# A fused linear-attention and feed-forward kernel: first rows of w loaded apart, w2 cast by its own load, and a new written-out order of the steps

## The chip, the cores and the metric

The kernel runs on one core of one Trainium2 chip. The metric is the device time of one execution in microseconds (us). TensorE (PE) multiplies matrices and writes PSUM; its weight loads (PEld) run beside its multiplications. VectorE (DVE), ScalarE (ACT) and GpSimd (POOL) do elementwise work, and GpSimd cannot read PSUM. DMAs move data between the chip's main memory and SBUF on 16 shared DMA engines. They are issued here by SyncE (SP), which does nothing else, by ACT in between its own instructions, and, in the changed kernel, by GpSimd too.

## The reference, cut to what matters

The first part is a linear attention with a decayed state, per batch b and head h; the second is a layer norm and a two-layer feed-forward block with a residual.

```python
# B, H, S, D = 4, 8, 768, 48
for t in range(S):
    kt, vt, rt = k[:, :, t], v[:, :, t], r[:, :, t]
    cur = einsum('bhd,bhe->bhde', u[None] * kt, vt)
    y[:, :, t] = einsum('bhd,bhde->bhe', rt, state + cur)
    state = w[None, :, :, None] * state + einsum('bhd,bhe->bhde', kt, vt)
x = y.transpose(0, 2, 1, 3).reshape(B, S, 384)
mu, var = mean(x, -1), mean((x - mu) ** 2, -1)
xn = (x - mu) / sqrt(var + 1e-06) * g_ln
out = x + maximum(xn @ w_ch1, 0) @ w_ch2        # w_ch1: 384x1536, w_ch2: 1536x384
```

## The kernel before, in words

The sequence is cut into 24 chunks of 128 positions (6 in each of 4 batches). Everything is a list of small steps, `PLAN`, a text of entries "name,number,engine" that is written out by hand or by a search outside the kernel. The loop at the end walks through it and emits each step. Every engine runs its own steps strictly in the order in which they stand; the text thus fixes five queues, and all DMAs also keep the order of the text among themselves. The engine letter is v for DVE, s for ACT, g for POOL; a DMA step with "s" is issued by ACT, without it by SP.

DMAs from SP and ACT share eight completion semaphores in turn. So a DMA is not issued before the DMA that stands eight places ahead of it in the common order has landed, whichever engine issued that one. The instruction that issues waits, and with it the queue of its engine.

The steps that the text speaks of, in the order of the work on one chunk i:

- LK, LV, LR load k, v, r of a chunk (192 KB each); KA/KB and RA/RB load k and r of a chunk in two "packed" halves of 96 KB. kf, rf and vf have ten slots each.
- SK, SR multiply k and r by powers of the decay (`Fk`, `Fkp`, `Fr`, `Fn`); CV casts v.
- TR transposes both on PE into one PSUM tile; TCr and TCk copy the two halves to `trs`. Later chunks have this done by transposing DMAs (TKD, TKR). For chunks 0 to 3, TB and KC transpose k back.
- Q multiplies the two; AT makes the scores on PE, AM (AMa, AMb in halves) masks them on DVE; S makes the state update and the u-term on PE; CC and VB form the u-term; ZU (and ZD) decay the state; Y makes the attention output on PE; X adds the u-term on DVE.
- SQ and XN center the row and sum its squares, RS makes the reciprocal root on POOL. LT (PE) and XT (copy), or the transposing DMAs LT2 and LTD, make `xT`.
- UP multiplies by w1 (12 or 6 matmuls a step, two PSUM tiles `hp` in turn); RL is the relu into `hT`, on ACT or DVE. DN multiplies by w2: four steps of four matmuls a chunk, the d-th of which reads `w2_sb[d]` (d from 0 to 2), and `hT`. OT (DVE) scales, adds the residual and writes `ot`, STO stores it. `ot` has four slots, the PSUM tile of DN one.
- In the feed-forward part, chunks 0 to 5 and 20 to 23 go alone, those between in pairs.

Before the first chunk can start, the decay powers are made. LC,0 loads w into `rows` (a tile of 11 x 128 that MW fills with ones first, since the 48 values of a head stand in a field of 64); LN takes the logarithm on ACT; WBR spreads it over the partitions on PE; PW, ER and EK (DVE) multiply it by positions, FR and FKP (ACT) take the exponentials. In the same way BD, WBK, FN and FK make the unpacked powers, and CT and CP turn w, u and g into columns for UW, WL and UGC.

The weights: LW1 loads w1 in three parts (n = 0, 1, 2), and nine SW steps scale them by -g into bf16 tiles `w1_sb`, on ACT, DVE and POOL. LW2 loads w2 in three parts of 768 KB as f32 into `w2_f`, and six CW steps cast them to bf16 into `w2_sb` (two each on POOL, DVE and ACT). The 31 DU steps are dummy matmuls on PE.

Lines of the profile: L236 WBR, L248 and L250 LC, L226 LN, L309 DU, L371 LW1, L388 LW2, L378/L380/L382 SW, L211/L213 copies and casts on ACT/DVE and POOL, L216 products (Q, SK, SR, Z), L400 packed loads, L396 LK, L427 LV, L448 and L452 TR, L479 AT, L489 AM, L523 S, L560 Y, L567 X, L574 SQ, L580 XN, L599 LT2, L611 TKD, L631 UP, L647/L649 RL on ACT/DVE, L659 DN, L715 OT, L722 STO.

Of the kernel before, what the change touches and what calls it, by code (L numbers as in the profile page):

```python
# [18 lines left out]
SLOTS = {'kf': 10, 'rf': 10, 'vf': 10, 'sc': 3, 'vv': 4, 'trs': 3, 'q': 2, 'A': 2, 'cc': 4, 'Z': 6, 'ZS': 2, 'Vb': 3, 'x': 13, 'xn': 4, 'xT': 4, 'hT': 4, 'ot': 4}  # L19
# [16 lines left out]
AM,5,v VB,4,v UP,48,- DN,8,- TR,6,- DN,9,- UP,50,- S,5,- TCk,6,v X,4,v TCr,6,s CC,5,v RL,48,v SK,8,g SR,8,g DN,10,- SQ,4,s
CV,5,s VB,5,g CV,6,s XN,4,s AT,6,- OT,2,v TR,8,- Y,5,- UP,49,- AM,6,v TCk,8,s X,5,v DN,12,- TCr,8,s RL,49,v LK,9,- RB,10,s
RL,50,s Q,6,g SR,7,v XN,5,v AT,8,- Y,6,- LT,4,- S,6,- DN,13,- XT,4,s SK,7,g LV,9,- RA,10,- RA,13,- LT,5,- UP,64,- XT,5,v
SQ,3,s RS,4,g Q,8,v CC,6,s SR,9,g RS,3,g STO,0,- TR,7,- DN,14,- ZU,6,v AM,8,v OT,3,v UP,80,- RL,64,s TCr,7,s CV,7,s TCk,7,s
UP,66,- Q,7,v AT,7,- VB,6,g SK,9,g TR,9,- S,7,- AM,7,v ZU,7,v X,6,v CC,7,v RL,80,s TCk,9,s TCr,9,s DN,16,- UP,65,- LK,10,-  # L40
RA,15,- LV,8,- RB,11,- RB,13,- SR,10,g Q,9,v VB,7,v ZD,7,v AT,9,- Y,7,- CV,9,g RL,66,s RL,65,s SK,10,g XN,6,s CV,8,s TR,10,-
UP,81,- X,7,v SR,11,v DN,17,- XN,7,s TCr,10,s S,8,- LK,11,- SQ,5,s RL,81,s DN,18,- ZU,8,v TCk,10,v CC,8,v RA,12,- LK,12,- UP,82,-
OT,4,v SK,11,g S,9,- TR,11,- DN,20,- ZD,8,g AM,9,v ZU,9,v VB,8,v CC,9,v Y,8,- SR,13,g DN,21,- RS,5,g LV,10,- LV,13,- RL,82,s
STO,1,s TCr,11,s AT,10,- CV,10,s SQ,6,s LT2,6,- RB,14,- RB,12,- X,8,v ZD,9,g SK,12,g VB,9,g LK,14,- LV,11,- DN,22,- Y,9,- UP,96,-
LK,13,- SQ,7,s TCk,11,v SR,12,g RA,16,s UP,97,- AM,10,v RB,15,- AT,11,- RL,96,v XN,8,s Q,10,v X,9,v RL,97,s UP,99,- S,10,- Y,10,-
UP,101,- LV,12,- RA,14,- OT,5,v TR,12,- XN,9,g SQ,9,s RL,99,s RL,101,s UP,98,- CC,10,v ZU,10,v Q,11,v UP,100,- DN,24,- SK,14,g SK,13,g
TCr,12,s TCk,12,s RL,100,s S,11,- LT2,8,- VB,10,g RB,16,- STO,5,- TR,13,- AM,11,v SR,14,v LK,15,- RS,6,g CV,12,v RL,98,s ZD,10,g TCr,13,s
# [12 lines left out]
RL,165,v TKR,20,- LR,22,- X,17,v AM,18,v CV,19,v DN,48,- UP,162,- S,18,- STO,8,s XN,17,s SQ,15,s CC,18,s DN,49,- AT,19,- DN,50,- Q,19,v  # L60
ZU,18,v OT,12,v S,19,- UP,164,- Y,18,- RL,162,s AM,19,v DN,52,- VB,18,g SK,22,g LT2,16,- UP,161,- STO,9,- CV,20,s CC,19,s ZU,19,v X,18,v
# [16 lines left out]
def kernel(  # L78
# [316 lines left out]
    def LK(i, e):  # L395
        nc.sync.dma_start(out=kf(i)[:], in_=chunk_src(k, i))  # L396
# [375 lines left out]
```

## Time and profile before

| | |
|---|---|
| median of 3 runs | 154.98 us (153.17 to 155.23) |
| profiled execution | 154.51 us, its span 152.4 us |
| granted TensorE clock, mean | 0.985 |
| bytes moved, read and written in main memory | 27.75 MB; 18.88 MB, 4.72 MB |

"Span" runs from the first to the last instruction; about 2 us lie around it. Shares and busy times are those of the page of the profile, which describes one execution. In its second part the span is cut into 40 slices of 3.8 us, with the busy share of each engine in tenths. The chain of waits follows the work that ended last back through what released it.

### The profile page before, as it was taken

The numbers are of one execution on the slowest core, as the hardware profiler recorded it, in microseconds if no ns is written. First come the engines' busy times: TensorE is split into PE (matmuls) and PEld (weight loads), VectorE is DVE, ScalarE is ACT, GpSimd is POOL, SyncE is SP. The second block draws the span as 40 slices with busy tenths as digits, with TensorE's granted clock in tenths as the row PEclk, the third lists the DMA queues.
The fourth block names the chain that finished last, engine by engine and source line by source line (L and its number), as shares of the span: only waits on it lengthen the run. The fifth ranks groups of instructions, "written<-read, shape, count | busy, mean of one in ns | idle before, by whom it ended". The sixth has DMA issues, their size and how long they took to land.

```text
span 152.4 us, 4469 instructions
## 1 busy us (share of the span) xinstructions
PE 142.4 (93%) x1755; PEld 109.8 (72%) x1755; DVE 120.9 (79%) x247; ACT 80.8 (53%) x178; POOL 90.9 (60%) x129
## 2 busy tenths in 40 slices
PE   7669799999999999999997899999999999999991
PEld 1235388786878887989785778887777787888880
DVE  0585889969997989999885989997999697674631
ACT  3226787977197787697545373666463514331010
POOL 5216526842999939999997057694839917622000
PEclk9995999999999999999999999999999999999998
DMA  5999998798686857959799599999888894042103
GB/s 179 244 232 305 369 426 240 159 217 192 133 215 139 195 114 176 225 150 242 124 175 203 124 185 215 182 214 176 217 181 162 193 209 147 3 131 85 48 14 141
DMA packets 79394, 27.75 MB, mean 182 GB/s; under 512 B 69003, under 2 KB 77838, under 8 KB 79374
## 3 DMA queue, kind: packets, MB, share of 16 engines
q1 hardware_dynamic: 77040, 25.11, 70.7%
q10 hardware_dynamic: 2334, 2.36, 4.8%
q8 instruction: 13, 0.21, 0.6%
q14 instruction: 7, 0.06, 0.1%
HBM read 18.88 MB, written 4.72 MB: 155 GB/s over the span
## 4 chain that ended last, share of the span: by engine, by line
PE 76%; DMA 12%; DVE 4%; SPq 2%; ACT 1%; issue 1%; POOL 1%; DVEq 0%; ACTq 0%
PE o L659 29%; PE hp L631 29%; DMA w_f<-in_moe_w_ch_dram 4%; PE at L479 4%; DMA out_dram<-ot 3%; PE y L560 3%; DMA vf<-in_v_dram 2%; DMA rows<-in_w_dram 2%; PE y L552 2%; PE tr L448 2%; PE s L523 2%; PE tr L452 2%; PE s L510 1%; SPq L400 1%; DVE w_sb L213 1%; ACT w_sb L378 1%
## 5 line engine op out<-in xcount | busy, mean ns | idle before, releaser
L659 PE MATMUL o<-w_sb,hT 128*128 128x384 bf16 x276 | 55.7, 326 | 1.8 <-DVE ot L715 1.5
L631 PE MATMUL hp<-xT,w_sb 128*128 128x128 bf16 (+1 forms) x612 | 57.1, 241 | 0.0
L631 PEld LDWEIGHTS <-w_sb 128*128 128x128 bf16 x612 | 48.8, 113 | 4.1
L647 ACT ACTIVATE hT<-hp 128x512 bf16<-128x512 f32 x51 | 29.8, 596 | 30.7 <-PE hp L631 22.1
L659 PEld LDWEIGHTS <-hT 128*128 128x128 bf16 x276 | 24.1, 98 | 12.8 <-issue 1.7
L489 DVE TENSOR_TENSOR A<-at,mask 128x1024 bf16<-128x1024 f32 (+1 forms) x27 | 29.7, 1099 | 2.1 <-PE at L479 2.0
L216 POOL TENSOR_TENSOR q<-trs 128x512 bf16<-128x512 bf16 x13 | 15.1, 1165 | 15.4 <-PE s L510 4.8
L715 DVE SCALAR_TENSOR_TENSOR ot<-o,rs,x 128x384 f32<-128x384 f32 x23 | 14.1, 615 | 10.8 <-PE o L659 7.9
L211 ACT COPY trs<-tr 128x512 bf16<-128x512 bf16 x25 | 13.8, 585 | 10.6 <-PE tr L452 3.3
L216 POOL TENSOR_TENSOR sc<-kf,Fk 128x384 bf16<-128x384 f32 x15 | 15.9, 1064 | 3.8 <-PE s L523 3.6
L542 POOL TENSOR_TENSOR Vb<-vf,cc 128x384 f32<-128x384 f32 x16 | 13.7, 858 | 7.4 <-ACT cc L211 3.9
L574 ACT ACTIVATE sqj<-x,sm 128x384 bf16<-128x384 f32 x24 | 14.8, 615 | 3.9 <-DVE x L567 3.3
L649 DVE TENSOR_SCALAR hT<-hp 128x512 bf16<-128x512 f32 x21 | 14.3, 688 | 2.0 <-PE hp L631 1.6
L567 DVE SCALAR_TENSOR_TENSOR x<-y,Vb 128x384 f32<-128x384 f32 x24 | 13.2, 550 | 2.1 <-PE y L560 1.6
L309 PE MATMUL o<-warm 128*128 128x512 bf16 x31 | 11.3, 468 | 1.1 <-DVE warm L264 1.1
L580 ACT ACTIVATE xn<-x,sm 128x384 bf16<-128x384 f32 x13 | 7.9, 611 | 7.3 <-DVE x L567 7.3
L591 POOL TENSOR_TENSOR rs<-rs,expo 128x1 f32<-128x1 f32 (+1 forms) x17 | 10.9, 642 | 1.4
L216 POOL TENSOR_TENSOR sc<-rf,Fr 128x384 bf16<-128x384 f32 x9 | 10.0, 1114 | 0.9 <-DMA rf<-in_r_dram 0.9
L479 PE MATMUL at<-trs 48*128 48x128 bf16 x192 | 9.8, 222 | 0.0
L479 PEld LDWEIGHTS <-trs 48*128 48x128 bf16 x192 | 5.6, 95 | 5.0 <-issue 3.9
L211 ACT CAST vv<-vf 128x384 bf16<-128x384 f32 x14 | 7.1, 513 | 3.9 <-DMA vf<-in_v_dram 3.1
L560 PE MATMUL y<-vv,A 128*128 128x48 bf16 x192 | 8.9, 183 | 0.1
(100 smaller groups left out, 190.0 us busy)
## 6 DMA issues: line engine op xcount, KB each, us to landing
w_f<-in_moe_w_ch_dram SPq DMA_DIRECT2D x6, 768.0 KB, 7.7
vf<-in_v_dram SPq DMA_DIRECT2D x24, 192.0 KB, 3.5
kf<-in_k_dram SPq DMA_DIRECT2D x20, 192.0 KB, 3.6
rf<-in_r_dram SPq DMA_DIRECT2D x30, 96.0 KB, 3.1
out_dram<-ot SPq DMA_DIRECT2D x15, 192.0 KB, 3.3
out_dram<-ot ACTq DMA_DIRECT2D x8, 192.0 KB, 3.1
rf<-in_r_dram SPq DMA_DIRECT2D x6, 192.0 KB, 3.6
kf<-in_k_dram SPq DMA_DIRECT2D x7, 96.0 KB, 3.4
```

The lines of the kernel that those rows point to most:

```text
L211: nc.scalar.copy(out=out, in_=in_)
L216: engines[e].tensor_tensor(out=out, in0=in0, in1=in1, op=ALU.mult)
L479: nc.tensor.matmul(out=t[:, par, q, :], lhsT=trs(i)[p0 : p0 + D, 1, q, :], rhs=trs(i)[p0 : p0 + D, 0, q, :], start=True, stop=True,)
L489: nc.vector.tensor_tensor(out=AA(i)[:, a:b].rearrange("p e q t -> p (e q) t"), in0=psum["at", i][:, a:b].rearrange("p e q t -> p (e q) t") ...
L542: engines[e].tensor_tensor(out=Vb(i)[:].rearrange("p (h d) -> p h d", h=H), in0=vf(i)[:], in1=cc(i)[:].unsqueeze(2).to_broadcast([P, H, D] ...
L560: nc.tensor.matmul(out=t[:, h * D : (h + 1) * D], lhsT=AA(i)[:, par, q, :], rhs=vv(i)[:, h, :], start=first, stop=True, skip_group_check=True,
L574: nc.scalar.activation(out=sqj[:], in_=xx(i)[:], func=ACT.Square, bias=sm[i][:], scale=-float(C), accum_out=sq[g][:, j : j + 1])
L631: nc.tensor.matmul(out=t[:, a * gw : (a + 1) * gw].rearrange("p (j t) -> p j t", j=size), lhsT=w1_sb[n][kc][:, fb::FB], rhs=xT(g)[:, :size ...
L647: nc.scalar.activation(out=o, in_=s, func=ACT.Relu)
L649: nc.vector.tensor_relu(out=o, in_=s)
L659: nc.tensor.matmul(out=psum["o", i][:, :C], lhsT=hT(g)[:, fk, j * P : (j + 1) * P], rhs=w2_sb[d][:, a, :], start=(fk == 0), stop=(fk == FK ...
L715: nc.vector.scalar_tensor_tensor(out=ot(i), in0=psum["o", i][:, :C], scalar=rs[g][:, j : j + 1], in1=xx(i)[:], op0=ALU.mult, op1=ALU.add,)
```

## The change

- LC,0 still loads w into `rows`, for the columns. But a new step LE, the first of the text, loads w once more into a tile of its own, `w_rows` of 4 x 96 (two heads of 48 in a row, no gap), from SP. LN reads that; `ln_rows` shrinks from 129 to 97 columns, and BD, WBR, PW and the spreading products with it.
- The three LW2 loads and the six CW casts are gone, and with them the f32 staging tiles. Three steps IW2, DMAs issued by GpSimd that read f32 and write bf16, put w2 straight into `w2_sb`. They take none of the eight semaphores.
- `hT` gets six slots in place of four.
- LK, LR and LV may be issued by ACT. ACT issues 47 DMAs in place of 18, among them LV,0, KA,0, KB,0, LV,1 and KA,2 at the start.
- The text of `PLAN` is a new one, 888 entries in place of 894, with 30 dummies in place of 31. The attention and feed-forward steps are the same in kind and number; their order and many engines are not. On DVE: Q 20 (was 11), SK 11 (8), SR 8 (14), RL 17 (21), CC 11 (18), ZD 2 (5), TCr and TCk 4 (7), XN 3 (4). On POOL: Q 4 (13), SR 16 (10), SK 13 (16), CV 9 (4), ZD 10 (7), XN 5 (7).

The core of the diff:

```diff
-SLOTS = {..., 'hT': 4, 'ot': 4}
+SLOTS = {..., 'hT': 6, 'ot': 4}
 PLAN = """
-MW,0,v LC,0,s TL,0,s DU,4,- LW2,1,- KB,1,- LC,2,s DU,4,- DU,4,- LN,0,s MI,0,g MM,0,g CW,3,g RB,1,- RA,0,- LV,1,- DU,4,-
-DU,4,- RB,0,- KA,0,- KB,0,- RA,1,s LC,1,s DU,4,- WBR,0,- DU,4,- PW,0,v ER,0,v LV,0,- KA,1,- LV,2,- RA,2,- FR,0,s EK,0,v
-MP,0,v FKP,0,s RB,3,- RB,2,s DU,4,- DU,4,- KB,2,s RA,3,s SR,0,v DU,4,- KA,3,- LW1,0,- KA,2,- DU,4,- DU,4,- LW1,2,- SK,0,v
...
+LE,0,- MW,0,v DU,4,- DU,4,- RA,0,- RB,0,- KB,1,- LV,0,s DU,4,- TL,0,s MM,0,g LC,0,s KA,3,- MI,0,g KA,0,s KB,0,s DU,4,-
+MP,0,v RA,1,- DU,4,- DU,4,- LN,0,s WBR,0,- KA,1,- RA,2,- KB,2,- RB,2,- LC,2,- DU,4,- IW2,1,g PW,0,v BD,0,v CV,0,v EK,0,v
+ER,0,v FKP,0,s LV,1,s DU,4,- WBK,0,- DU,4,- DU,4,- RB,1,- SK,0,v DU,4,- DU,4,- FR,0,s FK,0,s SR,0,v TR,0,- DU,4,- LC,1,s
+FN,0,s KA,2,s LW1,0,- LW1,2,- TCr,0,s DU,4,- DU,4,- TCk,0,s SR,1,v Q,0,v DU,4,- TB,0,- LW1,1,- SK,1,g DU,4,- CT,0,- DU,4,-
+AT,0,- KC,0,s CP,0,v TR,1,- LV,2,- RA,3,- UW,0,g S,0,- WL,0,s SK,2,g KB,3,- RA,5,- RB,3,- LV,3,- SR,2,v AMa,0,v RB,4,-
+LK,4,- TCk,1,s TCr,1,s UGC,0,s RB,5,- AMb,0,v ZU,0,v DU,4,- Y,0,- DU,4,- TB,1,- Q,1,v CC,0,s KC,1,v AT,1,- TR,2,- DU,4,-
+DU,4,- CV,1,s VB,0,g LK,5,- AMa,1,v SW,0,s SW,1,s X,0,v DU,4,- S,1,- DU,4,- DU,4,- AMb,1,v TCr,2,s TCk,2,s SW,2,s XN,0,v
+ZU,1,v CC,1,s SW,7,v SQ,0,s SW,8,s DU,4,- DU,4,- LT,0,- SW,6,g XT,0,v Y,1,- AT,2,- DU,4,- AMb,2,v VB,1,g SW,5,g X,1,v
+SW,4,s TB,2,- DU,4,- UP,0,- RL,0,s KC,2,v SW,3,v CV,2,v UP,2,- XN,1,s IW2,0,g Q,2,v AMa,2,v UP,1,- LT,1,- DU,4,- S,2,-
+RL,2,s SK,3,v SR,3,v XT,1,s RS,0,g IW2,2,g RL,1,s CC,2,s ZU,2,v VB,2,v Y,2,- UP,18,- TR,3,- SQ,1,s RL,18,s TCk,3,s X,2,v
+UP,16,- UP,17,- RA,4,s XN,2,s RL,16,s TCr,3,v DN,0,- LT,2,- AT,3,- Q,3,v DN,1,- XT,2,s TB,3,- UP,33,- DN,2,- RL,17,v CV,3,s
...
+    w_rows = const.tile([HP, E2], FP32, name="w_rows")
-    ln_rows = const.tile([HP, P + 1], FP32, name="ln_rows")
+    ln_rows = const.tile([HP, E2 + 1], FP32, name="ln_rows")
...
     def LN(i, e):
-        nc.scalar.activation(out=ln_rows[:, :P], in_=rows[:HP, :], func=ACT.Ln)
+        nc.scalar.activation(out=ln_rows[:, :E2], in_=w_rows[:], func=ACT.Ln)
+
+    def LE(i, e):
+        issuer(e).dma_start(out=w_rows[:], in_=w.rearrange("(q e) d -> q (e d)", e=2))
...
+    def IW2(n, e):
+        nc.gpsimd.dma_start(out=w2_sb[n][:], in_=w2_src[:, n])
+
     def LK(i, e):
-        nc.sync.dma_start(out=kf(i)[:], in_=chunk_src(k, i))
+        issuer(e).dma_start(out=kf(i)[:], in_=chunk_src(k, i))
...
```

More of the change, by code (lines that the diff above doesn't have):

```diff
@@ L200 @@
     w1_sb = [[const.tile([P, FW], BF16, name=f"w1_sb{n}_{kc}") for kc in range(CK)] for n in range(NW)]
-    w2_fl = [const.tile([P, FK // NW, C], FP32, name=f"w2_f{n}") for n in range(NW)]
+    w2_fl = [const.tile([P, FK // NW, C], FP32, name=f"w2_f{n}") for n in range(NW)] if "CW," in PLAN else None
     w2_sb = [const.tile([P, FK // NW, C], BF16, name=f"w2_sb{n}") for n in range(NW)]
@@ L236, in WBR @@
         nc.tensor.matmul(
-            out=t[:, : P + 1], lhsT=sel[:].rearrange("q k a -> q (k a)"), rhs=ln_rows[:], start=True, stop=True
+            out=t[:, : E2 + 1], lhsT=sel[:].rearrange("q k a -> q (k a)"), rhs=ln_rows[:], start=True, stop=True
         )
@@ L736 @@
     for ins in list(nc.cur_bb.bb.instructions)[traced:]:
-        chains = [ins.engine] + (["dma"] if "dma" in type(ins).__name__.lower() else [])
-        for chain in chains:
+        for chain in [ins.engine] + ["dma"] * ("dma" in type(ins).__name__.lower()):
             if chain in last:
-                tc.add_manual_dep(ins, last[chain].name, in_order, reason="program order")
+                tc.add_manual_dep(ins, last[chain].name, in_order, reason="order of the plan")
             last[chain] = ins
```

110 lines of the change are left out of this document (51 added, 59 removed).

## The prediction

> **What bounds the kernel now.** I read the page, then busy time by stretches, then the chain of waits, then single stages in the timeline. The page:
>
> ```profile
> span 152.4 us, 4469 instructions
> PE 142.4 (93%) x1755; PEld 109.8 (72%) x1755; DVE 120.9 (79%) x247; ACT 80.8 (53%) x178; POOL 90.9 (60%) x129
> ```
>
> Busy time by stretches (length, then PE, PEld, DVE, ACT, POOL, then clock, DMA share, GB/s), cut where the chain below changes its nature:
>
> ```profile
> 10.63:23.83 13.20, 12.24 (x144) 7.78 (x144) 10.37 (x25) 10.27 (x22) 7.24 (x9) 0.87 0.99 354
> 23.83:28.61 4.78, 4.34 (x74) 3.81 (x72) 4.43 (x10) 4.25 (x10) 3.49 (x5) 1.00 0.81 187
> 28.61:82.03 53.42, 53.29 (x765) 42.99 (x766) 48.81 (x99) 36.18 (x78) 43.06 (x52) 1.00 0.80 178
> 84.36:149.20 64.84, 64.84 (x740) 51.79 (x739) 51.28 (x95) 25.35 (x61) 31.94 (x44) 1.00 0.69 149
> ```
>
> From 28.61 on PE is never idle but in 82.03 to 84.36 and after 149.20. The change leaves PE's real work as it is. So it can win in two places only: before 28.61, and in that one hole. The chain of waits (start, length, what) shows what sets both:
>
> ```profile
> 1.00 3.63 DMA rows<-in_w_dram
> ...
> 4.67 0.60 SPq L400
> ...
> 5.97 3.75 DMA vf<-in_v_dram
> 9.72 0.02 issue
> 9.74 0.53 SPq L400
> 10.27 0.04 issue
> 10.31 6.76 DMA w_f<-in_moe_w_ch_dram
> ...
> 17.16 1.33 ACT w_sb L378 x2
> ...
> 20.50 0.67 PE hp L631 x12
> ...
> 27.51 1.05 DVE w_sb L213
> 28.56 0.05 issue
> 28.61 0.82 PE o L659 x4
> ```
>
> The reader sees the eight semaphores at work: the load of w lands at 4.63 and lets the next k load go at 4.67; a v load lands at 9.72 and lets SP go on at 9.74, which puts w1 at 10.31 and its landing at 17.07. Then ACT and DVE lead, and the last cast of the first third of w2 (CW,0) ends at 28.56, just before the first DN. The hole:
>
> ```profile
> 79.15 4.44 DMA out_dram<-ot
> 83.69 0.63 DVE ot L715
> 84.36 0.81 PE o L659 x4
> ```
>
> and the view of the waits, for PE:
>
> ```profile
> PE o L659 <- DVE ot L715: 1.5, 1, 1.5
> PE y L236 <- ACT ln_rows L226: 1.3, 1, 1.3
> ```
>
> A store (STO,4) left SP late, OT,8 had to wait for its slot, and PE lost 1.5 us. No longer wait of PE is in that view, and the next one lies in the start.
>
> **The change, part by part.** The start first, since it is a chain:
>
> ```profile
> 0.72 0.40 SPq L388 DMA_DIRECT2D w_f<-in_moe_w_ch_dram  x1
> 1.00 1.26 ACTq L250 DMA_DIRECT2D rows<-in_w_dram  x1
> 4.66 0.31 ACT L226 ACTIVATE ln_rows<-rows 4x128 f32<-4x128 f32 x1 [1.08 <-DMA rows<-in_w_dram]
> 8.70 0.58 ACTq L400 DMA_DIRECT2D rf<-in_r_dram  x1
> 10.63 1.07 ACT L211 COPY trs<-tr 128x512 bf16<-128x512 bf16 x2 [2.79 <-PE s L257]
> 23.83 1.09 ACT L647 ACTIVATE hT<-hp 128x512 bf16<-128x512 f32 x2
> ```
>
> *Logarithm of w.* LE leaves at 0.72 in place of 1.00, since no memset stands ahead of it. The old load landed 2.4 us after its 1.26 us of issue; so LE lands near 0.72 + 0.40 + 2.4 = 3.5. But on ACT the issue of KB,0 stands ahead of LN, and KB,0 is the eighth DMA after LE: it waits for LE's landing and then takes 0.6. So LN starts near 4.15, not at 3.5: 0.5 us earlier than 4.66. Bounds: 0.8 earlier, or 0.3 later if LE takes the old 3.63.
>
> *First copy of the transposes (TCr,0).* Now ACT runs FKP, the issue of LV,1, FR, FK, the issue of LC,1, FN and the issue of KA,2 ahead of TCr,0. From LN, DVE needs about 2.7 us (PW, BD, CV, EK and ER, with WBR in front) before FKP can start, near 6.9; FR waits for ER and LV,1's issue, 7.6; FK and FN of 0.55 each bring it to 9.2; KA,2, if its semaphore is free (KA,1 landed), to 9.6. So TCr,0 starts at 9.6 against 10.63, 1.0 us earlier. Bounds: 9.3, or 10.6 when KA,1 is late.
>
> *From there to the first DN.* ACT is the longest queue. In order of its steps up to the first relu (RL,0) stand six trs copies, five w1 scalings and about ten shorter steps. By the groups
>
> ```profile
> L378 ACT ACTIVATE w_sb<-w_f,g_neg x5: 706/707/733, 17.2 to 24.8; 128x512 bf16<-128x512 f32 x5
> L647 ACT ACTIVATE hT<-hp 128x512 bf16<-128x512 f32 x51 | 29.8, 596 | 30.7 <-PE hp L631 22.1 <-DVE ot L715 8.3
> ```
>
> that is 6 x 0.54 + 5 x 0.71 + 3.3 (four full steps at 0.60, the rest near 0.15 each) = 10.1 us. In the old stretch ACT was busy 10.27 of 13.20, idle 2.9; I take 1.0 of idle, since w1, issued near 9.3 when the eighth DMA before it lands, is there by 14 to 16 and no longer ends ACT's wait. RL,0 then starts at 9.6 + 10.1 + 1.0 = 20.7, against 23.83. From RL,0 to DN,0 stand eight more ACT steps (RL, XN, RL, XT, RL, CC, SQ, RL), 4.6 us at 0.60, and one UP of 0.67: DN,0 at 26.0. The old one was at 28.61, after the same six UPs and the same chunks. Gain 2.6 us. Bounds: idle of 0 and TCr,0 at 9.3 give 24.7, a gain of 3.9; idle of 2.9 and TCr,0 at 10.6 give 28.9, nothing. DVE's list to the same point is 0.5 to 0.7 us an instruction for some 28 instructions, about 16 us from 7.4: it ends by 24 and stays just under ACT.
>
> *w2 by casting loads.* Removed:
>
> ```profile
> L213 POOL CAST w_sb<-w_f x2: 816/819/822, 5.3 to 27.3; 128x768 bf16<-128x768 f32 x2
> L213 DVE CAST w_sb<-w_f x2: 576/845/1114, 26.3 to 27.4; 128x768 bf16<-128x768 f32 x2
> L211 ACT CAST w_sb<-w_f x2: 831/834/836, 28.7 to 30.0; 128x768 bf16<-128x768 f32 x2
> DMA to landing us min/median/max: 4.5/7.7/9.6
> ```
>
> 1.6, 1.7 and 1.7 us of three engines; those of DVE stood on the chain (27.51), and their gain is already in DN,0's 26.0. What comes instead has no row: a load by GpSimd that casts. IW2,0 stands behind SW,5 on POOL, which needs the third part of w1 (18.2 to 18.8) and 0.69 us of work: issue near 20. The nearest rows are the same bytes from SP: 4.5 us alone, 9.6 in the crowd. So w2's first third is there between 24.5 and 29.6, and DN,0 (26.0) waits 0 to 3.6 us. IW2,2, issued near 21.7, has until DN,2 near 28.7. I take no wait, nearest to the 4.5, since SP's crowd behind it is small packets. POOL spends some time on each issue, bounded by 0.58 (ACT's issue) and 3 us; it has that room, at 90.9 busy of 152.4.
> The Trainium skill ("DMA: Bandwidth & Descriptors", section "Anatomy of one DMA — SWDGE (gpsimd) path") fits 2.0 us plus bytes at 436 GB/s; for 768 KB its figure gives an estimate of 3.8 us, by which DN,0 would not wait either. No run here shows it yet.
>
> *Stores and the hole.* STO,4 goes to ACT's queue and stands some 9 us of PE work ahead of OT,8; the shortest such distance in the new order is 3.3 us (STO,16 to OT,20), against 1.6 in the old one. A store lands 3.3 us after issue:
>
> ```profile
> out_dram<-ot SPq DMA_DIRECT2D x15, 192.0 KB, 3.3
> xT<-xn SPq DMA_TRANSPOSE x11, 2.9
> L216 POOL TENSOR_TENSOR q<-trs 128x512 bf16<-128x512 bf16 x13 | 15.1, 1165 | 15.4 <-PE s L510 4.8 <-DMA rf<-in_r_dram 3.7 <-issue 3.1
> L216 DVE TENSOR_TENSOR q<-trs 128x512 bf16<-128x512 bf16 x11 | 5.7, 521 | 0.0
> L489 DVE TENSOR_TENSOR A<-at,mask 128x1024 bf16<-128x1024 f32 x21 | 25.6, 1218 | 1.5 <-PE at L479 1.3
> ```
>
> So the 1.5 us go; at worst they return elsewhere.
>
> *New engines, steady part.* Nine Q move from POOL (1.17 each) to DVE (0.52 each, +4.7); by its other moves DVE loses more, about 12 us in all counts, so it ends near 7 us lighter over the run. But not evenly: while PE does 9.4 us (from S,7 to UP,99) the new order gives DVE three masks of 1.22, four X, three Q, three ZU, two OT and six more, 14 us by their rows, some 12.4 with overlap. It lags by up to 3 us there. Likewise the way from Y over X, XN and a transposing DMA to UP needs 0.6 + 0.6 + 2.9 = 4.1 us, and has 4.7 to 5.1 of PE work beside it at UP,98, UP,128 and UP,148. New waits: 0 to 4 us; I take 1.0.
>
> *No price:* hT's two slots (in the old order a slot was written 9.8 us of PE work or more after its last reader), the shorter logarithm (4 x 96 for 4 x 128), one dummy less, and ACT's 29 more issues of 0.58 in the steady part: they run while ACT computes, and ACT is busy 25.35 of 64.84 late and 36.18 of 53.42 before. If that cover is gone, one that hits a relu costs 0.6.
>
> Sum: 154.5 (the profiled execution) - 2.6 - 1.5 + 1.0 = **151.4**. The profiled execution lies 0.5 below the median of 154.98; against that median it is -2.3%.
>
> **The rivals.**
> *The gain is given back.* DVE, not ACT, sets the start, or its lag after chunk 7 costs the upper bound: -2.6 - 1.5 + 4.0 gives 154.4; with half the start's gain, 153.6. For it: DVE was busy 48.81 of 53.42 in the old steady part. Against it: PE lost 0.13 us there all the same.
> *Slower: w2 comes too late.* The place is DN,0 and DN,2. If a casting load needs 9 us (the crowd's 9.6, rounded) and not 4.5, IW2,0 is there at 29, IW2,2, queued behind it, at 38; PE, which does everything in order, stands at DN,2 from 28.7 and loses 9.3 us: 160.7. It decides from 6 us a load on (32; 3.3 us lost, 154.7), and is slower by over 2% from 8 us on (36; 158.7). For it: no row shows such a load, and POOL, late itself, delays all three. Against it: fewer bytes are written, and nothing else uses that queue.
> The Trainium skill ("SBUF — State Buffer", section "SBUF: two separate sides") speaks against the change: while DVE copies in a mode that uses two ports, GpSimd cannot write the descriptors of its DMA. By DVE's copies and scalings of 0.35 to 0.48 near 20 us that would hold IW2,0 up by some 1.7 us and DN,0 by about half a microsecond; no trace here shows it yet.
> *ACT stands in its DMA queue.* KA,2, LC,1 or LV,1 wait for a slot while IW2,1's 768 KB fill the engines from 4 us on. Each microsecond shifts TCr,0 and all after it; with 3 us the start gains nothing and the time is 154.
>
> **How the numbers follow.** Forecast 0.54, its own range 149.1 (the start's 3.9, no new waits) to 152.9 (the start's 1.3, with 1.2 of new waits); given back 0.18 (152.9 to 154.4); w2 late 0.17 (154 to 161, most of it above 157); ACT's queue 0.11 (152.5 to 156). The range 149.0 to 156.5 leaves out most of the late w2 and a tail below, 2 in 10. A measurement here tells about 2% from no change, so faster means below 151.9 and slower above 158.1. Of the forecast case some three quarters of its range lie below 151.9, 0.40, and a little of the other cases is added: faster 0.42. Slower is most of the late w2 and a tail of ACT's queue: 0.16. Within 2%: 0.42.
>
> **What the new profile would show.** LN at 4.15 and TCr,0 at 9.6; RL,0 near 20.7; DN,0 near 26.0 with no wait for a DMA; no wait of DN for OT over 1 us; PE's waits after DN,0 about 1 us in all, at UP,98, UP,128 or S,14. Wrong would be: DN waiting for `w_sb` from a DMA, ACT's rows opening behind DMA issues before 10 us, or POOL busy for over 3 us with one issue.

## The result, and the profile after

The changed kernel takes 160.55 us (median of 4 runs, 159.30 to 161.51) against 154.14 us (median of 4 runs beside it): a ratio of 1.040, 95% interval 1.034 to 1.046. It is slower. The forecast was 151.4 with a range of 149.0 to 156.5, so both the time and its side were missed. The profiled execution took 159.3 us, the one of before 154.5. Some executions of a kernel take over 1.5% longer than its fastest; medians and ranges include them, the ratios and their intervals leave them out.

The page after (busy time of each engine):

```profile
span 157.0 us, 4429 instructions
PE 145.0 (92%) x1754; PEld 110.8 (71%) x1754; DVE 115.1 (73%) x232; ACT 85.1 (54%) x189; POOL 86.6 (55%) x130
```

VectorE has 5.8 us less to do than before and TensorE the same real work, and yet the span is 4.6 us longer. Busy time by stretches says where. First the kernel after (TCr,0 to RL,0, RL,0 to DN,0, DN,0 to the last of the final DN parts; columns: length, then PE, PEld, DVE, ACT, POOL, clock, DMA share, GB/s), then the last of these stretches in the kernel before:

```profile
10.86:22.13 11.27, 10.79 (x127) 7.10 (x126) 8.63 (x22) 9.10 (x21) 5.28 (x9) 1.00 0.99 312
22.13:27.08 4.95, 4.93 (x93) 4.70 (x91) 4.65 (x12) 4.76 (x11) 1.38 (x3) 1.00 0.98 170
27.08:153.10 126.02, 119.82 (x1514) 95.46 (x1512) 96.86 (x182) 67.50 (x152) 75.60 (x101) 1.00 0.75 158
```

```profile
28.61:148.70 120.09, 118.46 (x1507) 95.15 (x1508) 100.56 (x194) 63.72 (x144) 77.11 (x98) 1.00 0.74 161
```

DN,0 starts at 27.1 and not at 28.6: the start did gain, 1.5 us. From DN,0 on the same PE work, but for one LT more, takes 126.0 us and not 120.1. PE stands idle for 126.02 - 119.82 = 6.2 us of it, before for 120.09 - 118.46 = 1.6 us. The rest of the 5.9 us, 1.3 us, is busy time. The matmuls did not run longer (the DN take 55.5 us in sum, before 55.7, the UP 52.3 in both), so they overlapped less. So the change lost its time behind DN,0, where the prediction had put +1.0 for new waits and -1.5 for the hole. The view of the waits, for PE:

```profile
PE hp L638 <- DMA xT<-xn: 3.2, 3, 2.0
...
PE at L486 <- DVE A L496: 0.9, 1, 0.9
PE o L666 <- DMA w_sb<-in_moe_w_ch_dram: 0.8, 1, 0.8
...
PE hp L638 <- DVE xT L214: 0.5, 1, 0.5
PE s L517 <- DVE q L217: 0.3, 1, 0.3
```

No DN waits for `ot` by more than 0.3 us: the hole is gone, as forecast. In its place stand three UP that wait for a transposing DMA (3.2 us), one place where VectorE is late (A and q, 1.2 us), and DN,2, which waits for its casting load. Two rows of the chain show the size of the two transfers that end waits (start, length):

```profile
22.99 7.87 DMA w_sb<-in_moe_w_ch_dram
...
87.33 5.23 DMA xT<-xn
```

And the early instructions of ScalarE in the timeline (start, length, and in brackets what it stood idle for):

```profile
4.07 0.28 ACT L227 ACTIVATE ln_rows<-w_rows 4x96 f32<-4x96 f32 x1 [1.61 <-issue]
8.90 0.74 ACTq L254 DMA_DIRECT2D rows<-in_u_dram  x1
9.69 0.58 ACT L334 ACTIVATE Fn<-s,pow_n 128x384 f32<-128x384 f32 x1 [1.24 <-DMA rf<-in_r_dram]
10.86 1.07 ACT L212 COPY trs<-tr 128x512 bf16<-128x512 bf16 x2 [0.59 <-PE tr L459]
```

The logarithm came at 4.07 (4.15 was forecast), but the load of u (LC,1) stood in ScalarE's queue until a load of r had landed, and FN, which stands behind it on the same engine, started 1.24 us late. TCr,0, the copy, was not held by that: its row says that it waited for PE's transposes, and what these waited for is told with the run that moves IW2,1.

### The profile page after: what moved, and what is told of

It is laid out like the page before. It is cut to its first block, busy times and chain, and to the rows that moved or that the text cites. A ratio compares the mean times of both kernels' runs of the same rounds, so it can differ in the third digit from the quotient of the medians.

```text
span 157.0 us, 4429 instructions
## 1 busy us (share of the span) xinstructions
PE 145.0 (92%) x1754; PEld 110.8 (71%) x1754; DVE 115.1 (73%) x232; ACT 85.1 (54%) x189; POOL 86.6 (55%) x130
## 4 chain that ended last, share of the span: by engine, by line
PE 54%; DMA 26%; DVE 9%; issue 3%; ACT 2%; POOL 1%; SPq 1%; ACTq 0%; DVEq 0%
PE hp L638 23%; PE o L666 19%; DMA xT<-xn 12%; DMA w_sb<-in_moe_w_ch_dram 5%; DMA w_f<-in_moe_w_ch_dram 3%; DVE A L496 3%; DMA kf<-in_k_dram 2%; DMA rf<-in_r_dram 2%; PE at L486 2%; DMA out_dram<-ot 2%; PE y L567 2%; ACT xn L587 2%; DVE q L217 2%; PE y L559 1%; PE tr L455 1%
## 5 line engine op out<-in xcount | busy, mean ns | idle before, releaser
L666 PE MATMUL o<-w_sb,hT 128*128 128x384 bf16 x276 | 55.5, 326 | 1.1 <-DMA w_sb<-in_moe_w_ch_dram 0.8
L654 ACT ACTIVATE hT<-hp 128x512 bf16<-128x512 f32 x55 | 32.7, 596 | 32.7 <-PE hp L638 29.1
L496 DVE TENSOR_TENSOR A<-at,mask 128x1024 bf16<-128x1024 f32 (+1 forms) x27 | 29.6, 1099 | 1.2 <-PE at L486 0.8
L212 ACT COPY trs<-tr 128x512 bf16<-128x512 bf16 x28 | 15.6, 589 | 5.8 <-PE tr L459 5.3
L217 POOL TENSOR_TENSOR sc<-rf,Fr 128x384 bf16<-128x384 f32 x12 | 12.2, 1023 | 10.8 <-PE o L666 8.3
L217 POOL TENSOR_TENSOR Z<-ZS,WLZ 128x384 bf16<-128x384 f32 x10 | 10.6, 1056 | 9.9 <-DVE ZS L543 9.9
L217 POOL TENSOR_TENSOR sc<-kf,Fk 128x384 bf16<-128x384 f32 x11 | 11.8, 1075 | 6.2 <-PE s L530 3.3
L656 DVE TENSOR_SCALAR hT<-hp 128x512 bf16<-128x512 f32 x17 | 11.6, 686 | 4.3 <-PE hp L638 4.1
L587 ACT ACTIVATE xn<-x,sm 128x384 bf16<-128x384 f32 x16 | 9.8, 616 | 8.9 <-DVE x L574 4.9
L313 PE MATMUL o<-warm 128*128 128x512 bf16 x30 | 12.3, 521 | 1.1 <-DVE warm L268 1.1
L217 DVE TENSOR_TENSOR q<-trs 128x512 bf16<-128x512 bf16 x20 | 11.9, 596 | 0.6 <-ACT trs L212 0.6
```

The lines of the kernel that those rows point to most:

```text
L212: nc.scalar.copy(out=out, in_=in_)
L217: engines[e].tensor_tensor(out=out, in0=in0, in1=in1, op=ALU.mult)
L496: nc.vector.tensor_tensor(out=AA(i)[:, a:b].rearrange("p e q t -> p (e q) t"), in0=psum["at", i][:, a:b].rearrange("p e q t -> p (e q) t") ...
L587: nc.scalar.activation(out=xn(i), in_=xx(i)[:], func=ACT.Identity, bias=sm[i][:], scale=-float(C))
L654: nc.scalar.activation(out=o, in_=s, func=ACT.Relu)
L666: nc.tensor.matmul(out=psum["o", i][:, :C], lhsT=hT(g)[:, fk, j * P : (j + 1) * P], rhs=w2_sb[d][:, a, :], start=(fk == 0), stop=(fk == FK ...
```

## The experiments

Three theories went in. A: the loads and stores that ScalarE now issues hold up its computing, and run beside the transposing DMAs. B: the casting loads crowd the other loads. C: the order leaves too little PE work between Y and UP. D, that VectorE is too full ahead of S,11, was added after the first four runs, and E, that the start is good and the order behind DN,0 loses the time, after the next four. All ratios are to the kernel before, run beside on the same chip; its median was between 153.1 and 155.6 in the six sessions.

### ScalarE's DMAs given back to SyncE (twice)

```diff
- RA,4,s ... RB,8,s ... LV,4,s ... STO,22,s
+ RA,4,- ... RB,8,- ... LV,4,- ... STO,22,-      (40 steps)
```

> The changed kernel, but from chunk 4's first load of r on, the loads and stores that ScalarE issues are issued by SyncE, at the same places of the order (40 of its 48 DMAs; the early ones up to KA,2 stay on ScalarE). Theory A (ScalarE's own DMA issues, which wait for a slot, hold up its computing, and its late small packets make the transposing DMAs of 2.6 us take 5.2 to 5.5): the waits of PE at S,11 and AT,12 (1.5 us) and at UP,148 and UP,177 (3.3 us) go, and the time falls by 3 to 5 us, to 155.5 to 157.5. Theory B (the casting loads crowd the queues): those waits stay, time within 1 us of the changed kernel, 159.5 to 161. Theory C (the order leaves too little between Y and UP, DVE lags): the same, 159 to 161, with PE still waiting for xT at UP,148 by over 1.5 us.

Measured: 158.47 us (155.22 to 161.01) beside 155.58. The four executions lie too far apart for a ratio, and the granted clock of the profiled one was 0.967. What is read from its profile is that PE's waits for A and q at S,11 and AT,12 stayed (0.9 and 0.5 us), that UP,148 still waited 1.2 us, and that UP,177 waited no more; from DN,0 on it takes 123.8 us. Theory A is half right: right on UP,177, wrong on S,11. The same edit was made again on top of the run with IW2,1 later, which is told below:

> The run with IW2,1 later, and from chunk 4's first load of r on the 40 loads and stores of ScalarE are issued by SyncE at the same places of the order. If ScalarE's issuing beside SyncE's is what stretches the transposing DMAs for UP,148 and UP,177, their 3.4 us of waits fall below 1.5 and the ratio to the kernel before goes from 1.020 to 1.005 or 1.012; if the order alone leaves too little room, the waits stay or come back at other places and it stays at 1.015 to 1.025. S,11 and AT,12 keep their 1.5 us in both cases, since they wait for VectorE.

Measured: 156.23 us, 1.014 (1.006 to 1.023), against 1.020 (1.013 to 1.027) without the edit. The intervals overlap, so the gain is not settled by time alone. In the profiles, DN,0 to the end of the DN parts falls from 126.0 to 123.4 us, near the 123.8 of the first time: UP,177's wait is gone, UP,148 still waits 1.4 us, UP,128 has a new wait of 1.2 us, and S,11 and AT,12 don't wait either, which the expectation had excluded. Why they don't is in the section on the hardware.

### One part alone in the old order

The casting loads:

```diff
- LW2,1,- ... CW,3,g ... LW2,0,- ... LW2,2,- ... CW,1,v ... CW,0,v
+ IW2,1,g ...            IW2,0,g ... IW2,2,g
```

> The kernel before with one part of the change alone: the three loads of w2 are casting loads of GpSimd at the same places of the order, and the six casts and the staging are gone. Theory B (casting loads crowd the early loads): DN,0 or DN,2 waits for a DMA, loads issued beside them take 6 to 9 us, and the time is 155 to 158, over the kernel before. Theories A and C (the loads themselves are harmless): 1 to 2 us are gained, since the casts of 1.1 and 0.6 us on DVE ahead of DN,0 fall away: 152.5 to 154.

Measured: 158.67 us, 1.024 (1.014 to 1.034). Theory B was right on the sign and wrong on the place. No DN waits for w2; the price is paid by the first transposes, whose k and r come late:

```profile
PE tr L455 <- DVE sc L216: 2.3, 1, 2.3
```

The casting loads stand at 1.23 and 4.33 us there and land after 5.1 and 6.4 us; a load of k issued at 4.04 beside them lands after 6.9 us. DN,0 starts at 32.1. From DN,0 on nothing is lost (119.8 us).

The rows of w:

```diff
+ LE,0,- MW,0,v LC,0,s TL,0,s ...        (LN reads w_rows, 4 x 96)
```

> The kernel before with the rows of w loaded first by SyncE as 4 rows of 96 and the logarithm over these alone; four hT slots, everything else and the whole order as before. All theories: the logarithm starts 0.5 us earlier; the start is set by the loads (DMA share 0.99), so 0 to 0.5 us are gained: 153.5 to 154.5. One more DMA in the row of eight semaphores may shift who waits for whom by up to 1 us either way.

Measured: 155.49 us, 0.997 (0.990 to 1.004): no difference, as expected. Two things were not expected. DN,0 stands at 30.9 in this profile, 2.3 us later than before. And the hole at STO,4 and OT,8 is gone (118.8 us from DN,0 on), though no store moved. So in the profile the equal time is a loss and a gain that nearly cancel. One more DMA ahead shifts every later one by a place in the row of eight semaphores. That suggests that the hole was an accident of that row; no run tried it by itself.

### More PE work ahead of UP

```diff
- UP,98 UP,96 DN,22 | UP,128 DN,32    | UP,148 ... Y,15 DN,40 ... DN,41 | UP,177 ... DN,60 ... DN,61
+ DN,22 UP,98 UP,96 | DN,32 UP,128    | Y,15 DN,40 DN,41 UP,148         | DN,60 DN,61 UP,177
```

With the last of these, S,20 and OT,14 change their places by a few steps too.

> The changed kernel with more PE work ahead of the four UP groups that waited for a transposing DMA: DN,22 before UP,98, DN,32 before UP,128, Y,15 with DN,40 and DN,41 before UP,148, DN,60 and DN,61 before UP,177. All DMAs keep their places and engines. Theory C (the order leaves too little between Y and UP): most of the 3.9 us that PE loses at these four places go, less some 0.6 for OT waits, and the time falls by 2.5 to 3.5 us, to 157 to 158. Theory A: part of it goes, but the delay comes from loads and ScalarE and shows up again at the next steps (S, DN): 159 to 160.5. Theory B: as A.

Measured: 162.91 us, 1.052 (1.040 to 1.065): slower still. None of the four UP waits for its DMA any more, and from DN,0 on it still takes 126.7 us, since PE loses as much elsewhere:

```profile
PE o L666 <- DVE ot L722: 2.6, 3, 1.3
...
PE o L666 <- DMA w_sb<-in_moe_w_ch_dram: 1.3, 2, 0.9
```

The o bank in PSUM is one buffer: a DN that is pulled forward stands right behind the DN of the chunk before it and waits for that one's OT on VectorE. Theory C, in the form that a little more distance would do, has fallen.

### What w2's way is worth in the new order

> The changed kernel with four hT slots in place of six, all else the same. If the slots have no price in this order, 160 to 161; if the new order lives on them (up to three groups of UP stand ahead of the DN that free a slot), the relu steps wait and it is 1 to 5 us slower. Control for the run above.

Measured: 163.06 us, 1.046 (1.036 to 1.055), and 126.2 us from DN,0 on against 126.0: the two hT slots have no price that these runs can tell. The run serves as the control for the next, which has w2 by SyncE and six casts, with four slots:

> The changed kernel with w2 loaded as before: three float32 loads by SyncE into staging (the first where the casting load stood, the others behind the last load of w1 and the load of v for chunk 3) and six casts (four on GpSimd, one on VectorE, one on ScalarE). There is no room for six hT slots beside the staging, so it has four. Theory B (casting loads crowd the start): TR,0 begins by 10 us and not at 10.2 to 11.8, DN,0 and DN,2 don't wait for a DMA, and the time is 1.5 to 3 us under the changed kernel, 157.5 to 159. Rival (the casts on the engines cost as much as the crowding): DN,0 no earlier, 160 to 161.5.

Measured: 161.36 us, 1.038 (1.030 to 1.046). TR,0 begins at 9.5 and not at 12.7 as in its control, no DN waits, and 1 us comes out of it at DN,0 (28.6 against 29.6). The intervals of the two overlap. The rival was nearly right on the time, but the profile doesn't show the casts as its cause. The longest new wait on the way is VectorE's, for a load of r beside the first part of w2, which SyncE issues at 8.1 us, and w1:

```profile
14.17 0.56 DVE L217 TENSOR_TENSOR sc<-rf,Fr 128x384 bf16<-128x384 f32 x1 [4.78 <-DMA rf<-in_r_dram]
```

SR,1 starts at 14.2 there and at 13.3 in the control, though TR,0 came 3.2 us earlier. So the crowd moved from k to r; what the casts cost beside it, no run tells apart.

### The first casting load later

```diff
- LC,2,- DU,4,- IW2,1,g PW,0,v ...  SK,2,g KB,3,-
+ LC,2,- DU,4,- PW,0,v ...          SK,2,g IW2,1,g KB,3,-
```

> The changed kernel with the first casting load (IW2,1) moved behind the scaling of k for chunk 2 on GpSimd, from 3 us to about 14 us, when the first chunks' loads have landed. Theory B (it crowds the first loads): the load of u is no longer held, TCr,0 starts at 9.6 to 10.0, DN,0 about 1 us earlier, 158.5 to 160, if the w1 loads beside which it now runs don't come later by as much. Rival (the crowd only moves): TR,0 earlier, but the last third of w1 and RL,0 late by as much, 160 to 162.

Measured: 158.52 us, 1.020 (1.013 to 1.027), against 1.040 (1.034 to 1.046) for the changed kernel: the intervals are apart, so 2% or some 3 us of the loss hung on this one place. ScalarE's early rows:

```profile
7.88 0.72 ACTq L254 DMA_DIRECT2D rows<-in_u_dram  x1
8.65 0.58 ACT L334 ACTIVATE Fn<-s,pow_n 128x384 f32<-128x384 f32 x1 [0.21 <-issue]
10.46 1.07 ACT L212 COPY trs<-tr 128x512 bf16<-128x512 bf16 x2 [1.23 <-PE tr L459]
```

The load of u is held no more, and FN starts 1.0 us earlier than in the changed kernel's profile. But FN is only a sign. TCr,0 waits for PE's transposes here and in the changed kernel, and these wait for the scaled k and r of chunk 0, SK,0 and SR,0 on VectorE. SK,0 needs the load KB,0, issued at 3.3 us. Its rows with IW2,1 at 3 us (in the first run with SyncE's issues, whose early order is that of the changed kernel) and in this run:

```profile
9.50 0.56 DVE L217 TENSOR_TENSOR sc<-kf,Fkp 128x384 bf16<-128x384 f32 x1 [2.53 <-DMA kf<-in_k_dram]
```

```profile
7.38 0.56 DVE L217 TENSOR_TENSOR sc<-kf,Fkp 128x384 bf16<-128x384 f32 x1
```

By the traces KB,0 landed at 8.6 to 10.7 us in the six profiles with IW2,1 at 3 us (8.63 in the changed kernel's), and SK,0 started 0.1 us later, at 8.71 to 10.79. In the seven profiles of this start without it there, KB,0 landed at 6.2 to 7.0 and SK,0 started at 7.38 to 7.40. So the casting load's price in the start is paid by the load of k, which lands 2 to 4 us later, and through it by SK,0, 1.3 to 3.4 us later. The changed kernel's profile is the mildest of the six: DN,0 starts at 27.1 to 30.0 in them, and at 26.3 to 26.8 in the four profiles that differ from this run only behind DN,0 or not at all. The crowd did not merely move: RL,0 came at 21.73 and DN,0 at 26.70. Behind DN,0 nothing changed: 126.0 us.

### VectorE and the transposing DMA, together and apart

> The changed kernel with two local edits. (1) Ahead of S,11 and AT,12: the cast of v for chunk 11 and the relu of UP,100 move from VectorE to ScalarE, and the load LK,13 and the store STO,2 from ScalarE to SyncE, so that ScalarE is free for them. Theory D (VectorE is full there, its copies and products stretched to 1.0 to 1.2 us beside GpSimd's): the 1.7 us of PE waits at S,11, AT,12 and DN,24 fall below 0.5. Theory A (ScalarE stuck in its DMA queue) says the same of the move of the two DMAs alone, but the run with SyncE issues has already kept those waits. (2) The loads LR,19, LV,19 and LK,19 stand behind UP,145, 3 us later, so that they don't run beside the transposing DMA for UP,148. If contention is what stretched it, it lands after 2.6 to 3.5 us and not 5.2, and the 2.1 us wait at UP,148 is under 0.7; if not, the wait stays. Both together: 157.5 to 158.5.

```diff
- CV,11,v ... RL,100,v ... LK,13,s ... STO,2,s ... LR,19,s (around XN,12) LV,19,s LK,19,s
+ CV,11,s ... RL,100,s ... LK,13,- ... STO,2,- ... RL,145,s LR,19,s LV,19,s LK,19,s
```

Measured: 163.91 us, 1.050 (1.040 to 1.060). Both waits went, as said: S,11 and AT,12 wait no more, and UP,148 starts 3.2 us after its DMA's issue and does not wait. And both came back: UP,128 waits 2.2 us for its transposing DMA, and S,16 waits 1.9 us for the cast of v. The two halves, each alone, on top of IW2,1 later:

> The run with IW2,1 later, and one edit: the loads LR,19, LV,19 and LK,19 of ScalarE stand behind RL,145 and not around XN,12. If loads beside it stretch the transposing DMA for UP,148, it lands 2.6 to 3.2 us after issue (4.9 without the edit), the 1.7 us wait at UP,148 is under 0.5, and the time falls by 1 to 1.7 us, to 157. If the wait comes back behind it (S,16 waited 2.0 us for the cast of v when these loads stood ahead of it on ScalarE), the time stays at 158 to 159. If contention isn't the cause, the wait stays at 1.7.

Measured: 158.94 us, 1.033 (1.025 to 1.041); no gain. UP,148 now waits 0.3 us and not 1.7, so it was those three loads that stretched its DMA, from 3.5 us after issue to 4.9. But ScalarE now issues them ahead of the cast of v for chunk 16, and there a store stands 3.0 us in its queue (the first two rows are the timeline, the third PE's waits):

```profile
92.86 3.01 ACTq L729 DMA_DIRECT2D out_dram<-ot  x1
95.91 0.51 ACT L212 CAST vv<-vf 128x384 bf16<-128x384 f32 x1 [2.48 <-issue]
```

```profile
PE s L530 <- ACT vv L212: 2.7, 1, 2.7
```

> The run with IW2,1 later, and one edit: the cast of v for chunk 11 and the relu of UP,100 go from VectorE to ScalarE, the relu ahead of ScalarE's load LK,13. Theory D (VectorE is behind there): the 1.74 us of waits at S,11, AT,12 and DN,24 fall below 0.4 and the time falls by 1 to 1.7 us, to 157; or they come back at UP,128, whose transposing DMA then runs beside other loads (2.4 us in the earlier run): 158 to 159. If it is ScalarE's issuing and not VectorE, the waits stay.

Measured: 158.82 us, 1.029 (1.019 to 1.038); no gain. The 1.7 us at S,11, AT,12 and DN,24 are gone (S,10 to DN,24 takes 5.6 us and not 7.3), so VectorE's two steps were the cause there. It comes back downstream: UP,148 waits 2.3 us in place of 1.7, and AT,20 has a new wait:

```profile
PE hp L638 <- DMA xT<-xn: 2.6, 2, 2.3
...
PE at L486 <- DMA trs<-sc: 0.9, 1, 0.9
```

### Orders, engines and issuers exchanged

> The kernel before with its order and all its compute as it is; only the issuer of its loads and stores from chunk 4's load of r on is that of the changed kernel (45 DMAs change between SyncE and ScalarE, ScalarE then issues some 45). Theory A (issuing by ScalarE costs): ScalarE stands behind slots, relu and XN steps come late, transposing DMAs run beside more small packets, 157 to 159. Theory E without A: 155 to 156, as before.

Measured: 164.64 us, 1.072 (1.063 to 1.081), and theory A's size is right for a reason that it did not have. Behind DN,0 nothing is lost at all (119.7 us). All of it is one wait in the start:

```profile
27.08 1.45 ACTq L400 DMA_DIRECT2D rf<-in_r_dram  x2
28.58 1.33 ACT L378 ACTIVATE w_sb<-w_f,g_neg 128x512 bf16<-128x512 f32 x2 [9.40 <-DMA rf<-in_r_dram]
```

Two loads of r, now ScalarE's, waited for a slot until 27 us, and the scaling of w1 behind them on the same engine stood 9.4 us; PE stood 8.6 us with it.

> The kernel before with its order and its DMAs as they are; behind DN,0 each compute step is on the engine that the changed kernel uses (115 steps move: eight Q from GpSimd to VectorE, 27 relus between ScalarE and VectorE, scalings, casts, XN). Theory D (the engines are the cause: VectorE's products of two SBUF tiles are stretched beside GpSimd's): PE waits for q, A and ot as at S,11, 157 to 160. Theory E (the order, not the engines): 154.5 to 157.

> The changed kernel with its order; behind DN,0 each step, DMAs too, is on the engine or issuer of the kernel before (160 steps). Theories A and D (engines and issuers are the cause): the 6 us behind DN,0 mostly go, 155.5 to 157.5. Theory E (the order itself, how close X, XN, the transposing DMA and UP stand): they stay, 159.5 to 163.

Measured: 168.89 us, 1.099 (1.086 to 1.111) and 168.94 us, 1.097 (1.085 to 1.109). The stretch from DN,0 on takes 134.8 and 133.6 us, where each order with its own engines takes 120.1 and 126.0. So putting the old engines and issuers into the new order does not take its loss away, and the new engines in the old order lose more than the change did: by these two runs each order lives on its own engines. All theories missed both, by 6 to 12 us from the near end of their ranges.

### The new start with the old rest

> The order of the run with IW2,1 later up to and with DN,0, and behind it all steps that are left in the order and on the engines of the kernel before (six hT slots, casting loads, w rows first). Theory E (the start is good once the first casting load is out of the way, and the 6 us are lost in the order behind DN,0): DN,0 at 26.7, 120 us from there to the last DN part, 152 to 153.5 in all, faster than both kernels. Rival (the early start is borrowed: 20 loads that the old order issues ahead of DN,0 now come later): PE waits for loads or scalings behind DN,0, 155 to 157.

Measured: 152.40 us (10 runs), 0.992 (0.987 to 0.998). In its profile, of an execution of 154.4 us, DN,0 stands at 27.2, half a microsecond of it spent waiting for IW2,0, then follow 120.3 us. Theory E holds: the start was not borrowed. What is left of the wait at DN,0 is the aim of the last edit:

```diff
- SK,2,g IW2,1,g ... IW2,0,g ... IW2,2,g
+ SK,2,g IW2,0,g ... IW2,1,g ... IW2,2,g
```

> The new start with the old rest, and IW2,0 and IW2,1 change places, so that the third that DN,0 needs is issued near 14 us and that of DN,1 near 20. If DN,0 waited for the order of the loads, its 0.6 us go and the time is 151.5 to 152.5 or 0.98 to 0.99 of the kernel before; if the load at 14 us crowds w1 all the same or DN,1 now waits as long, no change, 0.99.

Measured: 152.33 us (6 runs), 0.988 (0.983 to 0.994): 1.2% under the kernel before, which its interval bears out, though it is less than the 2% that a measurement here tells from no change, and some 5% under the changed kernel. The intervals of this run and the one before it overlap, so the gain of the exchange itself is not settled by time. The stretch from DN,0 on in its profiled execution (151.5 us):

```profile
25.90:145.52 119.62, 118.98 (x1513) 95.32 (x1512) 101.23 (x194) 63.64 (x144) 76.11 (x95) 1.00 0.80 166
```

DN,0 starts at 25.9, no DN waits for w2, and PE idles 119.62 - 118.98 = 0.6 us in that stretch.

## Why the prediction was wrong

**The logarithm:** 4.07 for 4.15, but by luck. The step had LE landing near 3.5 and the issue of KB,0 waiting for it. By the trace LE landed at 2.1 us and held up nothing. What LN waited for is ScalarE's queue itself, which issued LC,0 (1.35 us from 1.22 on) and then KA,0 and KB,0 (1.42 us from 2.60 on) until 4.02; the issue of LC,0 ahead of these two was not in the sum.

**The first copy (TCr,0) at 9.6:** wrong, 10.86. The step followed ScalarE's list alone and left out the other chain to the same copy: the load of k, VectorE's SK,0 and SR,0, PE's transposes. With IW2,1's bytes under way that chain was the later one, since KB,0 landed at 8.63. The rival "ACT stands in its DMA queue" came true as an event, LC,1 did wait for a slot, but FN ended at 10.3 and TCr,0 went on waiting for PE until 10.86. With that load moved, FN ended at 9.2 as worked out, and TCr,0 still started at 10.46, behind PE. 0.8 us of that is SR,0, which takes 1.35 us beside a product of GpSimd and 0.55 without (the section on the hardware).

**DN,0 at 26.0:** 27.1 measured, 26.7 with IW2,1 moved and 25.9 with the loads in the order of need. The way from TCr,0 to DN,0 came out right (16.4 us forecast, 16.2 measured), with luck in its terms: from TCr,0 to RL,0 ScalarE was busy for 9.1 us and not 10.1, and idle for 2.2 and not 1.0. The other five profiles with IW2,1 at 3 us, with DN,0 at up to 30.0, suggest that the median run of the changed kernel kept less of the gain than its profile.

**w2 by casting loads, no wait:** nearly. IW2,0 took 5.0 us (4.5 was taken) and DN,0 did not stand. IW2,2 took 7.9, and DN,2 lost 0.8 us by the view of the waits. The rival with both loads queued behind each other did not come; its price of 9 us a load was too high. What the forecast left unpriced was the third load, IW2,1, at 3 us: its cost is not where w2 is needed but where k is. By the Trainium skill ("DMA: Bandwidth & Descriptors", section "Anatomy of one DMA — SWDGE (gpsimd) path") the estimate was 3.8 us. The three took 5.3, 5.0 and 7.9 us, so the traces don't agree with it beside other traffic.

**The hole's 1.5 us:** gone, as forecast. The run with the rows of w alone shows that it goes without moving a store, too.

**New waits, 0 to 4, taken 1.0:** this is the step that failed. PE's idle time from DN,0 on grew from 1.6 us with the hole to 6.2 without it. It failed in three of its inputs. The transposing DMA was put at 2.9 us from a median, and it took 5.2 where three loads of ScalarE ran beside it; the three loads alone, moved, brought the wait at UP,148 from 1.7 to 0.3 us. VectorE's lag of up to 3 us after S,7 was seen and then given no price; two steps taken off it removed 1.7 us of PE's waits there. And ScalarE's 29 more issues (48 and not 19, with the last store) had "no price": in the profiles they are worth 2.2 to 2.6 us in the new order (126.0 against 123.8 and 123.4), though by time alone that isn't settled, and 0 behind DN,0 in the old one.

**The bound was wrong too.** "0 to 4" was drawn as if each wait stood for itself. Every local mending (more work ahead of UP, loads later, VectorE relieved) took its wait away and got most of it back elsewhere, with no gain in time in any of the four runs. Behind DN,0 the old order takes 119 to 120 us, the new one 125 to 128 with ScalarE's issues and 123 to 124 without, and the two exchanges of engines 134 and 135. What holds the new order as a whole, beyond these waits that replace each other and ScalarE's issues, stays open. One number of the first rival is also wrong as a sum: with half the start's gain its terms give 152.7 (new waits of 1.0) or 155.7 (of 4.0), not 153.6.

**No price for the hT slots:** right (126.2 against 126.0 us).

The outcome in sum: of a ratio of 1.040 some 2% hung on the place of one casting load. The rest is the order behind DN,0 with its engines and issuers: +5.9 us there, against 1.9 us won in the start once that load is out of the way.

## What to carry to other kernels

Price a load by who else is waiting for its engines at that time, not only by when its own data is needed: 768 KB issued at 3 us, beside the first k and r, cost some 3 us of the whole; at 15 us what could be seen of their cost was 0.5 us at DN,0 in one run, gone when the third that DN,0 needs went first. An engine that computes and issues DMAs pays for every slot that is not free with all the work behind it, so put such issues where their slot is surely free. When a written-out order, its engines and its issuers were made together, take or leave them as stages (here: all up to DN,0 from one, all behind it from the other), since three of the four exchanges tried (issuers, engines, engines with issuers) ended 7 to 10% above the kernel before. The fourth, SyncE's issues in the new order, cost nothing.

## What the runs showed of the hardware

VectorE's copies and products of SBUF tiles took two to three times as long when they started beside a GpSimd product that had begun first. The same three steps, in the same order, in the run with IW2,1 later and in the one with SyncE's issues on top. First VectorE and GpSimd in the former:

```profile
65.78 0.98 DVE L214 CAST vv<-vf 128x384 bf16<-128x384 f32 x1
...
67.82 1.18 DVE L549 TENSOR_TENSOR Vb<-vf,cc 128x384 f32<-128x384 f32 x1
68.92 1.23 DVE L217 TENSOR_TENSOR q<-trs 128x512 bf16<-128x512 bf16 x1
```

```profile
65.55 1.00 POOL L217 TENSOR_TENSOR sc<-rf,Fr 128x384 bf16<-128x384 f32 x1
...
67.57 1.01 POOL L217 TENSOR_TENSOR sc<-rf,Fr 128x384 bf16<-128x384 f32 x1
68.54 1.32 POOL L217 TENSOR_TENSOR sc<-kf,Fk 128x384 bf16<-128x384 f32 x1
```

and in the latter:

```profile
65.16 0.35 DVE L214 CAST vv<-vf 128x384 bf16<-128x384 f32 x1
...
66.56 0.55 DVE L549 TENSOR_TENSOR Vb<-vf,cc 128x384 f32<-128x384 f32 x1
67.03 0.41 DVE L217 TENSOR_TENSOR q<-trs 128x512 bf16<-128x512 bf16 x1
```

```profile
65.23 1.14 POOL L217 TENSOR_TENSOR sc<-rf,Fr 128x384 bf16<-128x384 f32 x1 [0.27 <-DMA rf<-in_r_dram]
...
66.72 0.94 POOL L598 TENSOR_TENSOR rs<-rs,expo 128x2 f32<-128x2 f32 x1
67.63 1.00 POOL L217 TENSOR_TENSOR sc<-rf,Fr 128x384 bf16<-128x384 f32 x1
```

In the former each step starts 0.2 to 0.4 us after a GpSimd product and ends 0.2 to 0.4 us after that one's end; in the latter the cast starts 0.07 us ahead of the product and the other two run beside a step of two elements a row, and all three keep their short times. The difference is 0.63 + 0.63 + 0.82 = 2.1 us of VectorE; in the former S,11 and AT,12 wait 0.4 and 0.9 us, in the latter neither does.

The start shows it from both sides. First SR,0 and GpSimd's SK,1 in the run with IW2,1 later, then in the changed kernel:

```profile
7.86 1.35 DVE L217 TENSOR_TENSOR sc<-rf,Fr 128x384 bf16<-128x384 f32 x1
7.65 1.14 POOL L217 TENSOR_TENSOR sc<-kf,Fkp 128x384 bf16<-128x384 f32 x1 [4.66 <-DMA kf<-in_k_dram]
```

```profile
9.18 0.55 DVE L217 TENSOR_TENSOR sc<-rf,Fr 128x384 bf16<-128x384 f32 x1
9.28 1.31 POOL L217 TENSOR_TENSOR sc<-kf,Fkp 128x384 bf16<-128x384 f32 x1 [5.54 <-DMA rf<-in_r_dram]
```

In the eleven profiles of this start in which SK,1 begins ahead of SR,0, by 0.03 us or more, SR,0 takes 1.34 to 1.38 us. In the two in which SR,0 begins first it takes 0.55, and SK,1 takes 1.31 and 1.40 us, where its least is 0.99.

This is what the Trainium skill says ("SBUF — State Buffer", section "SBUF: two separate sides"): the port pair that the two engines share is an exclusive lock, held for the whole instruction by whichever starts first, for a VectorE step in a two-port mode, or for one with two SBUF inputs against a GpSimd step that reads SBUF. The trace agrees. The prediction had used the same section for GpSimd's descriptors alone, where the runs show nothing of that size: GpSimd spent 0.6 to 0.8 us on each casting load. No run took only the GpSimd steps away, so the lock is read from the profiles and not tried by itself.

A DMA issue on ScalarE took mostly 0.4 to 0.7 us, and 3.0 us for the store at 92.86 us shown above, in which the profile names nothing that it waited for.
